# Input products of chunks 8 to 15 in two frames of 512 tokens, with the state inputs rotated in place

## The chip, the cores and the metric

The kernel runs on one core of one Trainium2 chip. The metric is device time in microseconds (us) of one execution; lower is better. The engines are PE (TensorE, matmuls), PEld (its weight loads), DVE (VectorE), ACT (ScalarE), POOL (GpSimd) and SP (SyncE, which starts transfers). Each works through its own queue in order. "L697" is line 697 of the kernel in question, so the same operation has different line numbers in different kernels. The granted clock is the share of TensorE's full clock that the chip allowed, as the profile records it. The record classes a run as slow when it is over 1.5% above the fastest of the same kernel.

## The reference, cut to what matters

```python
Bu = einsum("bld,pd->blp", layernorm(x), B_bar)     # L = 2048 tokens, D = P = 1024
for t in range(L):
    h = Lam_bar * h + Bu[:, t]                      # complex diagonal recurrence
y = 2 * einsum("blp,dp->bld", hs, C).real + layernorm(x) * Dskip
# ... plus: the two tokens with the highest x @ w_r go through a gated expert,
# y[those tokens] += sigmoid(r) * ((silu(xs @ w_gate) * (xs @ w_up)) @ w_down)
```

(Shortened: each branch is one line, the residual x + layernorm(x) is left out, and in the expert's line x is the normalised x, on which the kernel works.)

## The kernel before

The tokens are cut into 16 chunks of 128. For each chunk:

1. ScalarE normalises x (sum, sum of squares, rstd, apply). A transfer transposes it.
2. TensorE forms the input products u of a *frame* of two chunks: 8 groups, each of 16 matmuls of 256 columns. ScalarE moves each group from PSUM, where TensorE's results are written, into u: its *evacuation*.
3. VectorE rotates u into v, so that the complex recurrence becomes two real scans; scans v into gf (two buffers); ScalarE casts gf into gb, which frees gf; VectorE turns gb back into hT (the *turn back*).
4. TensorE forms the output products of hT; VectorE adds the residual (L863) and the chunk is stored.

In between, the router (r_bf and what follows it on VectorE) selects the two tokens, and TensorE runs the expert in 21 small steps, each with its own weights from HBM.

```python
def evac_u(f, j):                                    # ScalarE, one group of a frame of 2 chunks
    if j == 0:
        u_tiles[f] = work.tile([128, 2, PT, TF], BF16, name="u", bufs=2)
    nc.scalar.copy(out=u_tiles[f][:, :, j, :], in_=pB_tiles.pop((f, j))[:])

def turn_in(c, js=ALLJ):                             # VectorE, L697 to L699
    ...
    rot = v[:, :, js, 2:]
    nc.vector.tensor_tensor(out=rot, in0=u, in1=both(E1c, js), op=ALU.mult)
    nc.vector.tensor_tensor(out=m[:, :, js, :], in0=u[:, ::-1], in1=E1s[:, :, js, :], op=ALU.mult)
    nc.vector.tensor_add(out=rot, in0=rot, in1=m[:, :, js, :])

# scan, L718: v -> gf (two buffers); scan_out, L724, ScalarE: gf -> gb
```

The order of every queue is fixed when the program is built. A list scheduler in the kernel picks among the tasks that are ready by a priority key, and a long table `ADJUST` of hand-tuned shifts of these keys follows the kernel from version to version. So this change is also a change of the order on every engine.

## Time and profile before

| | before |
|---|---|
| time | 266.6 us (266.29 to 266.65) |
| profiled span | 264.4 us |
| busy: PE, DVE, ACT | 256.5, 251.5, 158.9 us |
| VectorE's waits of 0.3 us and more | 6.0 us, of which 2.3 at the start and 1.8 at the very end |
| granted TensorE clock | 1.0 |

How to read it: two engines have almost no free time, so neither can take up a delay of the other for long. From 20 to 258 us VectorE has no wait over 0.7 us. The prediction below shows the lines.

### The profile page before, as it was taken

To read this page: it belongs to the slowest core of one execution; us is meant where nothing else is said; L and a number is where in the kernel's file an instruction comes from. 1 tells how busy PE (TensorE), PEld (TensorE's weight loads), DVE (VectorE), ACT (ScalarE), POOL (GpSimd) and SP (SyncE) were. 2 spreads that over 40 slices of the span, in tenths; PEclk is the share of its full clock that TensorE was granted. 3 is DMA by queue.
4 is the path that set the end of the run, shared out by engine and by line. 5 is a ranking of instruction groups with operands and counts; after the bars stand their busy time and mean duration, and the time that the engine had idled before them with its cause. 6 is when DMAs were issued, how large, how long until landed. Compare 5 with 4: busy or idle time off the path is not lost.

```text
span 264.4 us, 5522 instructions
## 1 busy us (share of the span) xinstructions
PE 256.5 (97%) x2207; PEld 173.2 (66%) x2227; DVE 251.5 (95%) x334; ACT 158.9 (60%) x281; POOL 83.6 (32%) x126
## 2 busy tenths in 40 slices
PE   7799999999999999999999999999999999999994
PEld 7799988774688457456756586455864776644461
DVE  6999999999999999999999999999998999999992
ACT  3799999959699999996524447034551533145110
POOL 4221303563545440731040217115260409011100
PEclk9999999999999999999999999999999999999999
DMA  8999999998541125416111197588967884770411
GB/s 180 188 175 218 171 235 229 248 271 293 153 137 57 47 60 165 138 40 183 58 62 60 35 360 237 187 266 287 296 235 253 289 272 175 269 288 20 117 46 40
DMA packets 66165, 46.51 MB, mean 176 GB/s; under 512 B 45844, under 2 KB 52122, under 8 KB 66140
## 3 DMA queue, kind: packets, MB, share of 16 engines
q1 hardware_dynamic: 65788, 45.82, 63.4%
q8 instruction: 17, 0.28, 0.5%
q0 software_dynamic: 144, 0.27, 0.3%
q10 hardware_dynamic: 208, 0.07, 0.1%
q14 instruction: 8, 0.07, 0.1%
HBM read 30.94 MB, written 4.20 MB: 133 GB/s over the span
## 4 chain that ended last, share of the span: by engine, by line
PE 61%; DVE 28%; issue 3%; SPq 2%; ACT 2%; DMA 2%; DVEq 0%
PE pB L646 34%; PE pY L849 20%; DVE gf L718 9%; DVE ot L863 3%; PE pG L1048 3%; DVE hT L759 3%; DVE m L760 3%; DVE v L699 2%; DVE v L697 2%; DVE m L698 2%; DMA BT<-in_A_B_im_dram 2%; DVE gb L711 2%; SPq L286 2%; PE pD L1088 1%; PE pY L842 1%
## 5 line engine op out<-in xcount | busy, mean ns | idle before, releaser
L646 PE MATMUL pB<-xnT,BT 128*128 128x256 bf16 (+1 forms) x1104 | 117.5, 265 | 1.1 <-DMA BT<-in_A_B_im_dram 1.1
L849 PE MATMUL pY<-CT,hT 128*128 128x512 bf16 (+1 forms) x508 | 114.8, 372 | 1.7 <-issue 0.5
L646 PEld LDWEIGHTS <-BT 128*128 128x128 bf16 x1104 | 99.7, 98 | 16.2 <-issue 3.2
L849 PEld LDWEIGHTS <-hT 128*128 128x128 bf16 x528 | 49.1, 98 | 52.6 <-issue 3.2
L734 POOL TENSOR_TENSOR cw<-gf,tL 128x16 f32<-128x16 f32 (+1 forms) x38 | 35.0, 924 | 136.1 <-DVE gf L718 135.2
L718 DVE TENSOR_TENSOR_SCAN gf<-R,v 128x1040 f32<-128x1040 f32 (+1 forms) x38 | 69.0, 1851 | 0.2
L652 ACT CAST u<-pB 128x512 bf16<-128x512 f32 x64 | 36.5, 580 | 34.8 <-PE pB L646 34.7
L724 ACT CAST gb<-gf 128x1024 bf16<-128x1024 f32 (+1 forms) x38 | 32.4, 862 | 24.6 <-DVE gf L718 24.5
L810 ACT ACTIVATE xa<-xr,nmr_all,rstd_all 128x1024 f32<-128x1024 bf16 x12 | 14.9, 1239 | 21.9 <-DMA xr<-in_A_x_dram 8.1
L699 DVE TENSOR_TENSOR v<-v,m 128x2048 bf16<-128x2048 bf16 (+2 forms) x22 | 20.6, 938 | 0.8
L761 DVE TENSOR_TENSOR hT<-hT,m 128x2048 bf16<-128x2048 bf16 (+2 forms) x22 | 20.5, 934 | 0.8
L759 DVE TENSOR_TENSOR hT<-gb,E2c 128x2048 bf16<-128x2048 bf16 (+2 forms) x22 | 20.5, 930 | 0.2
L697 DVE TENSOR_TENSOR v<-u,E1c 128x2048 bf16<-128x2048 bf16 (+2 forms) x22 | 20.4, 928 | 0.2
L760 DVE TENSOR_TENSOR m<-gb,E2s 128x2048 bf16<-128x2048 bf16 (+2 forms) x22 | 20.5, 930 | 0.0
L698 DVE TENSOR_TENSOR m<-u,E1s 128x2048 bf16<-128x2048 bf16 (+2 forms) x22 | 20.4, 930 | 0.0
L863 DVE TENSOR_TENSOR ot<-pY,xa 128x512 bf16<-128x512 f32 (+1 forms) x25 | 16.0, 656 | 2.4 <-PE pY L852 1.8
L749 POOL CAST v<-cy 128x16 bf16<-128x16 f32 (+1 forms) x19 | 14.1, 744 | 1.4
L349 ACT ACTIVATE xn<-xt,nmean_all 128x1024 bf16<-128x1024 bf16 x12 | 13.8, 1149 | 0.3
L742 POOL TENSOR_TENSOR cy<-cw 128x16 f32<-128x16 f32 (+1 forms) x19 | 12.8, 674 | 1.5
L343 ACT ACTIVATE xn<-xt 128x1024 bf16<-128x1024 bf16 x12 | 12.6, 1054 | 0.0
L374 ACT ACTIVATE xn<-xt,nmr_all,rstd_all 128x1024 bf16<-128x1024 bf16 x10 | 12.4, 1241 | 0.3
L750 POOL TENSOR_TENSOR v<-cy,v 128x16 bf16<-128x16 f32 (+1 forms) x19 | 11.1, 586 | 1.5
(153 smaller groups left out, 186.6 us busy)
## 6 DMA issues: line engine op xcount, KB each, us to landing
wt<-in_B_w_up_dram SPq DMA_DIRECT2D x14, 512.0 KB, 5.1
wt<-in_B_w_gate_dram SPq DMA_DIRECT2D x14, 512.0 KB, 3.8
wt<-in_B_w_down_dram SPq DMA_DIRECT2D x14, 512.0 KB, 3.9
xt<-in_A_x_dram SPq DMA_DIRECT2D x16, 256.0 KB, 3.1
xr<-in_A_x_dram SPq DMA_DIRECT2D x16, 256.0 KB, 2.5
out_dram<-ot SPq DMA_DIRECT2D x31, 128.0 KB, 2.6
Drow<-in_A_Dskip_dram SPq DMA_DIRECT2D x1, 256.0 KB
xnT<-xn SPq DMA_TRANSPOSE x10, 2.8
```

The source lines that it names most:

```text
L646: nc.tensor.matmul(out=pB[:, ri, ts_], lhsT=BT[ri][j][:, k, :], rhs=xnT_tiles[f][:, k, ts_], start=(k == 0), stop=(k == DT - 1))
L652: nc.scalar.copy(out=u_tiles[f][:, :, j, :], in_=pB_tiles.pop((f, j))[:])
L697: nc.vector.tensor_tensor(out=rot, in0=u, in1=both(E1c, js), op=ALU.mult)
L698: nc.vector.tensor_tensor(out=m[:, :, js, :], in0=u[:, ::-1], in1=E1s[:, :, js, :], op=ALU.mult)
L699: nc.vector.tensor_add(out=rot, in0=rot, in1=m[:, :, js, :])
L718: nc.vector.tensor_tensor_scan(out=flat(gf), data0=flat(R[:, js, :]), data1=flat(v[:, ri, js, :]), initial=0.0, op0=ALU.mult, op1=ALU.add)
L724: nc.scalar.copy(out=gb_tiles[c][:, ri, js, :], in_=gf_tiles[c, js.start, ri][:, :, 2:])
L734: nc.gpsimd.tensor_tensor(out=cw_tiles[c, js.start][:, ri, :, 0:n], in0=g.unsqueeze(1).to_broadcast([128, 2, n]), in1=tL[:, ri, :, js], op ...
L759: nc.vector.tensor_tensor(out=rot, in0=g, in1=E2c[:, :, js, :], op=ALU.mult)
L760: nc.vector.tensor_tensor(out=m[:, :, js, :], in0=g[:, ::-1], in1=both(E2s, js), op=ALU.mult)
L849: nc.tensor.matmul(out=pY[:], lhsT=h_tiles[c][:, ri, j, :], rhs=CT[ri][h][:, j, d0:d0 + w], start=first and c in SKIP_DVE and ri == rs[0] ...
L863: nc.vector.tensor_add(out=y_tiles["ot", c][:, d_], in0=y_tiles.pop(("pY", c, dh))[:], in1=y_tiles["xa", c][:, d_])
```

## The change

The intent is to give TensorE longer matmuls (512 columns in place of 256, with half the weight loads) for the second half of the sequence. A frame of four chunks needs more of u at once. To make room, u and v are merged: six chunk slots, each written by ScalarE and rotated in place by VectorE; normalised x gets twelve chunk slots. Cut to its core:

```diff
-    CPF = TF // 128
+    CPF = 2
+    FRAMES = [(0, 1), (2, 3), (4, 5), (6, 7), (8, 9, 10, 11), (12, 13, 14, 15)]
+    NSLOT, NXS = 6, 12
...
+    u_all = work.tile([128, NSLOT, 2, PT, T + 2], BF16, name="u_all")
+    def stage_Bu1(f, j, ri):                         # 512 columns
+        for k in range(DT):
+            nc.tensor.matmul(out=pB[:], lhsT=BT[ri][j][:, k, :], rhs=xnT_all[:, k, x0:x0 + n], ...)
...
-        nc.vector.tensor_tensor(out=rot, in0=u, in1=both(E1c, js), op=ALU.mult)
         nc.vector.tensor_tensor(out=m[:, :, js, :], in0=u[:, ::-1], in1=E1s[:, :, js, :], op=ALU.mult)
-        nc.vector.tensor_add(out=rot, in0=rot, in1=m[:, :, js, :])
+        nc.vector.tensor_tensor(out=u, in0=u, in1=both(E1c, js), op=ALU.mult)
+        nc.vector.tensor_add(out=u, in0=u, in1=m[:, :, js, :])
...
-            cw_tiles[c, js.start] = small.tile([128, 2, 2, PT], F32, name="cw", bufs=3)
+            cw_tiles[c, js.start] = small.tile([128, 2, 2, PT], F32, name="cw", bufs=2)
...
 ADJUST = {                                           # every shift is new, among them:
+    ('gb', 5, 0, 0): 50.3, ('gb', 5, 0, 1): 150.6,
```

(Comments and "..." are mine; some 60 lines of shifts are left out.)

## The prediction

> **What bounds the kernel now.** I read the page first, then the chain that ended last in order of time, then the waits of VectorE, then VectorE's timeline. From the page, the busy times and the chain's shares:
>
> ```profile
> span 264.4 us, 5522 instructions
> PE 256.5 (97%) x2207; PEld 173.2 (66%) x2227; DVE 251.5 (95%) x334; ACT 158.9 (60%) x281; POOL 83.6 (32%) x126
> ...
> PE 61%; DVE 28%; issue 3%; SPq 2%; ACT 2%; DMA 2%; DVEq 0%
> ```
>
> TensorE and VectorE are both nearly full, and the chain changes between them: TensorE to about 59 us, VectorE from 66 to 118, TensorE to 232, VectorE to 258. So it is a balance of two full engines, and a saving on one alone is worth at most what the other has spare. What VectorE has spare is read from its waits:
>
> ```profile
> DVE ot L863 <- PE pY L852: 1.8, 2, 1.5
> DVE halfpi L237 <- PEq L1150: 0.8, 1, 0.8
> DVE st L334 <- DMA xt<-in_A_x_dram: 0.8, 1, 0.8
> DVE first_tok L243 <- POOL par_i L234: 0.7, 1, 0.7
> DVE guT L1077 <- PE pU L1068: 0.7, 1, 0.7
> DVE ot L863 <- PE pY L849: 0.5, 1, 0.5
> DVE row L918 <- PE pR L914: 0.4, 1, 0.4
> DVE E1s L615 <- ACT sf L545: 0.3, 1, 0.3
> ```
>
> Of these 6.0 us, 2.3 are the start, and 1.8 the last products at the end, which any order has. The rest, 0.7 + 0.5 + 0.4 + 0.3 = 1.9 us, is all that VectorE could give up. Its other 7 us of not-busy time (264.4 - 251.5 - 6.0) are the store after its last instruction (2.8 us) and small gaps between dependent instructions. Those gaps decide this case, and the timeline shows them:
>
> ```profile
> 101.09 2.31 DVE L718 TENSOR_TENSOR_SCAN gf<-R,v 128x1040 f32<-128x1040 f32 x1
> 103.32 1.26 DVE L863 TENSOR_TENSOR ot<-pY,xa 128x512 bf16<-128x512 f32 x2
> 104.50 2.31 DVE L718 TENSOR_TENSOR_SCAN gf<-R,v 128x1040 f32<-128x1040 f32 x1
> 106.85 1.23 DVE L697 TENSOR_TENSOR v<-u,E1c 128x2048 bf16<-128x2048 bf16 x1
> 107.99 1.25 DVE L698 TENSOR_TENSOR m<-u,E1s 128x2048 bf16<-128x2048 bf16 x1
> 109.27 1.23 DVE L699 TENSOR_TENSOR v<-v,m 128x2048 bf16<-128x2048 bf16 x1
> 110.41 1.22 DVE L759 TENSOR_TENSOR hT<-gb,E2c 128x2048 bf16<-128x2048 bf16 x1
> ```
>
> Columns: start, duration, engine, line, operation. An instruction that needs nothing of the one before starts before that one has ended: L698 comes 1.14 us after L697, although L697 lasts 1.23. One that needs it starts after its end: L699 comes 1.28 after L698 (1.25 to 1.26 in other chunks). A scan with an unrelated add behind it takes 2.23 us (101.09 to 103.32); a scan with a rotation behind it that overwrites the very v buffer just scanned takes 2.35 (104.50 to 106.85). The second pair carries no data from one to the other, only a buffer to be reused. So a wait on the instruction directly before costs about 0.12 us, whether for data or for a buffer.
>
> **What the Trainium skill says.** "TensorE: Matmul & The Clock Gate", section "Wait — 56ns, not 53.3ns?", gives a warm matmul of N columns a start-to-start time of N / 2.4 GHz plus about 2.5 ns. The trace agrees: in the chain 80 input products of 256 columns take 8.76 us, 109.5 ns each (formula 109.2), and 16 output products of 512 columns take 3.45 us, 215.6 ns each (formula 215.8). "VectorE: DVE Perf Modes", section "The DRAIN you can't avoid", says that a semaphore between two VectorE instructions costs nothing extra. This trace disagrees, by the 0.12 us above; I go by the trace. The section "Two Vector instructions with no wait between them" does say that unheld instructions may overlap. "Mode 2×_1P — pack two bf16 into one 32-bit read" asks for 4-byte alignment and step ±1; the new u slots begin at element 2 of rows of 130 bf16, so at 4 bytes, as v does already. L699, which reads and writes v in that layout, takes 1.22 us like the others, so I expect the in-place instructions to keep their durations.
>
> **The change, part by part.**
>
> TensorE. For chunks 8 to 15, 512 matmuls of 256 columns become 256 of 512. One pair saves 2 x 109.5 - 215.6 = 3.4 ns by the trace (2.5 by the formula): 256 pairs give 0.6 to 0.9 us. The 256 weight loads that vanish (98 ns each, 25 us of PEld) lay under matmuls of 109 ns and save nothing. Streamed columns are unchanged. Sum: -0.7 us.
>
> ScalarE. Still 64 evacuations of 512 elements (580 ns each). The normalisation of chunks up to 11 is now needed when frame 8 to 11 starts. In the kernel before, ScalarE wrote normalised chunk 11 at 91 us and chunk 15 at 117 us; the new order of ScalarE's queue puts chunk 11 behind nearly the same work, and I count frame 8 to 11 to start near 107 us on TensorE. So no wait there.
>
> VectorE. The number of instructions is the same (290 listed rows in both). What changes is who stands behind whom:
> - In the old rotation L697 wrote v and L698 read u: independent. In the new one the first instruction reads u into m, and the second overwrites u, so it must wait for the first. The built program has a wait on VectorE itself on this second instruction in all 22 rotations; it is always the direct neighbour. +22 waits.
> - m is now written by the first instruction, so it stands directly behind the last reader of m wherever a rotation follows another rotation or a turn back: 4 + 2 places. Before, an instruction lay between. +6.
> - A scan directly behind its own rotation: 4 places before, 6 now. +2.
> - The old rotation that waits for the scan just before it to free v: 6 places with such a wait. With six slots gone. -6.
> Sum: 24 waits of 0.12 us = 2.9 us more on VectorE.
>
> Buffers. Six slots instead of two u frames and two v buffers remove waits which the trace does not show anyway. The coarse frame asks for something instead: the first rotation of chunks 12 to 14 must follow all 16 groups of their frame. I summed both queues in their new order with the durations of this trace. From the first group of that frame, TensorE has 16 x 8 x 0.2156 = 27.6 us of it, with eight expert products between (8 x 0.55 = 4.4) and one small transpose pair: 32 us, from about 161 to 193.6. VectorE comes to chunk 12 at about the same time, 193.6. With 0.7 us for the evacuation it waits up to about 0.8 us there, where before it had a like wait of 0.7 for guT. Frame 8 to 11 ends about 137 us, a microsecond ahead of VectorE. After chunk 12 is ready, VectorE has 67 us of work and TensorE 64, so VectorE is the later one. These times are estimates, good to a microsecond or two.
>
> Sum on the path: VectorE +2.9, less what of its 1.9 us of waits the new order may avoid (I take 0.5); TensorE's 0.7 us falls on the engine that finishes earlier and is lost. 264.4 + 2.4 = 266.8 us of span, plus the 2.2 us between span and time (266.6 - 264.4): 269.0 us.
>
> **Rivals.**
> 1. TensorE is the bound and only its saving counts: 266.6 - 0.7 = 265.9, and with the waits of VectorE smoothed out by the new order perhaps 264.5. For it: 97% busy against 95%, and 61% of the chain. Against: the chain's last 26 us before the final products are VectorE's, and the trace shows less than 2 us that it could give up, so it cannot take up 2.9 us unseen.
> 2. The coarse frames open a new hole: VectorE waits for frame 12 to 15, or TensorE waits for evacuations that wait for the scan of chunk 9. If TensorE is late by 3 us at chunk 12, VectorE's remaining work ends 3 us later: 272. For it: my two sums meet within a microsecond. Against: the new order starts chunk 15's first parts before chunk 12, which need only 8 and 12 of the 16 groups, so whoever ordered it had seen this place.
> 3. The in-place waits cost only when VectorE is on the path. If half of them fall where TensorE is late, +1.4 and about 267.5. Against: VectorE has no gap over 0.7 us between 20 and 258 us, so a delay anywhere is carried to the end.
>
> **Range and chances.** Rival 1 gives the low side, rival 2 the high one. An order that was evidently searched anew for this kernel leans to the low side of my sum: I take 266.0 to 271.8. Faster by over 2% would be under 261.3; VectorE's own 251.5 busy, 2.3 start and 4.6 end leave a span of 258.4, a time of 260.6, as a floor with no gap at all: 2%. Slower by over 2% is over 271.9, needs rival 2: 9%. The rest, 89%.
>
> **What would show it.** Right: in the changed kernel's timeline the second instruction of every rotation starts 1.25 us or more after the first (before: 1.14), durations unchanged near 1.22; 512-column products 215 to 217 ns apart; VectorE in the chain for most of the last 70 us; TensorE with new idle time in the tail. Wrong: if the second instruction still starts at 1.14, my main cost is none; if VectorE's durations rise, the slots' layout costs; if VectorE waits over 2 us for input products, rival 2; if the span falls below 264, TensorE was the bound.

## The result, and the profile after

The time rose to 276.2 us (275.30 to 277.14, four runs), against 266.6. The ratio is 1.0367 (95%: 1.0332 to 1.0402). A ratio here is the mean time of one kernel's fast runs over that of the other's of the same rounds, so not quite the ratio of the medians quoted. The prediction said 269.0, at most 271.8.

The page of the kernel after, first lines and the chain's shares:

```profile
span 273.7 us, 5046 instructions
...
PE 257.5 (94%) x1971; PEld 147.9 (54%) x1971; DVE 253.5 (93%) x334; ACT 159.2 (58%) x281; POOL 80.9 (30%) x126
...
PE 51%; DVE 32%; ACT 5%; issue 5%; DMA 3%; SPq 2%; DVEq 0%
```

The span grew by 9.3 us, but TensorE's busy time by 1.0 and VectorE's by 2.0. The rest is waiting. VectorE's waits in the kernel after (waiter, line, what it waited for: us in total, times, longest):

```profile
DVE gf L753 <- ACT gb L759: 3.8, 2, 2.6
DVE ot L895 <- PE pY L884: 2.7, 2, 2.3
DVE hT L794 <- ACT gb L759: 1.6, 2, 1.1
DVE guT L1109 <- PE pU L1100: 1.1, 1, 1.1
...
DVE m L732 <- ACT u_all L680: 0.6, 2, 0.3
```

Two rows are new in kind: 3.8 + 1.6 = 5.4 us of waits for ScalarE's casts gf to gb, which the kernel before does not have. VectorE's timeline shows where (start, duration, engine, line, operation; in brackets the wait before it):

```profile
104.11 1.20 DVE L732 TENSOR_TENSOR m<-u_all,E1s 128x2048 bf16<-128x2048 bf16 x1
105.35 1.22 DVE L733 TENSOR_TENSOR u_all<-u_all,E1c 128x2048 bf16<-128x2048 bf16 x1
106.61 1.22 DVE L734 TENSOR_TENSOR u_all<-u_all,m 128x2048 bf16<-128x2048 bf16 x1
...
111.53 2.31 DVE L753 TENSOR_TENSOR_SCAN gf<-R,u_all 128x1040 f32<-128x1040 f32 x1
115.02 2.33 DVE L753 TENSOR_TENSOR_SCAN gf<-R,u_all 128x1040 f32<-128x1040 f32 x1 [1.18 <-ACT gb L759]
118.46 1.23 DVE L794 TENSOR_TENSOR hT<-gb,E2c 128x2048 bf16<-128x2048 bf16 x1 [1.11 <-ACT gb L759]
...
122.00 2.32 DVE L753 TENSOR_TENSOR_SCAN gf<-R,u_all 128x1040 f32<-128x1040 f32 x1
126.91 2.33 DVE L753 TENSOR_TENSOR_SCAN gf<-R,u_all 128x1040 f32<-128x1040 f32 x1 [2.60 <-ACT gb L759]
```

The first three lines are the in-place rotation: its second instruction starts 1.24 us after the first (104.11 to 105.35); before, it was 1.14. Over the 11 rotations of this size the medians are 1.25 and 1.13 us, and over all 22 rotations the difference sums to 2.5 us. Three of the last five lines carry new waits; a fourth, of 0.53 us, is at 96.13. ScalarE's timeline says why the cast for the last one was late:

```profile
118.33 1.55 ACT L680 CAST u_all<-pB 128x512 bf16<-128x512 f32 x3
119.76 1.08 ACT L356 ACTIVATE xn<-xt 128x1024 bf16<-128x1024 bf16 x1
...
123.55 1.24 ACT L387 ACTIVATE xn<-xt,nmr_all,rstd_all 128x1024 bf16<-128x1024 bf16 x1
...
124.88 1.05 ACT L680 CAST u_all<-pB 128x512 bf16<-128x512 f32 x2
125.82 1.05 ACT L759 CAST gb<-gf 128x1024 bf16<-128x1024 f32 x1
```

The cast at 125.82 is that of chunk 5's second scan, which had ended 21.6 us earlier, at 104.2 (101.90 + 2.30). It stands in ScalarE's queue behind the evacuations of frame 8 to 11 and the normalisation of chunk 15. The Trainium skill's page "TensorE: Matmul & The Clock Gate", section "Architectural detail: the array is 16× 32×32, not 1× 128×128", says that the queues of ScalarE and VectorE are strict FIFO. The trace agrees: the cast's input had been ready for 21.6 us, and it did not overtake. Until it came, one of the two gf buffers was held, and both scans of chunk 6 and the first of chunk 7 shared the other; the built program shows the same address for these three. The late place is no accident of the run. It is the shift 150.6 in the diff above: built with 50.3 in its place (not run), the scheduler puts this cast directly behind that of the first half.

The last view is the end of the two kernels, in windows. The columns are the window, its length, then busy us and instructions of PE, PEld, DVE, ACT and POOL, the granted clock, the DMA share and GB/s. Before:

```profile
220.00:240.00 20.00, 19.79 (x179) 10.38 (x179) 19.83 (x21) 6.92 (x10) 6.13 (x9) 1.00 0.64 227
240.00:258.00 18.00, 17.80 (x103) 9.20 (x103) 17.60 (x27) 4.45 (x5) 1.59 (x1) 1.00 0.20 60
```

After:

```profile
220.00:240.00 20.00, 17.66 (x125) 7.50 (x127) 19.67 (x17) 6.61 (x7) 9.16 (x10) 1.00 0.82 274
240.00:258.00 18.00, 15.39 (x122) 7.10 (x122) 17.77 (x17) 6.30 (x9) 4.50 (x5) 1.00 0.38 123
```

Before, both engines are full up to the end, because the input products of chunks 14 and 15 run as late as 207 to 227 us, between output products and expert steps. After, all input products are done at 198.7, and TensorE has only work that waits for VectorE: it is idle for 2.3 + 2.6 us here.

As sums on VectorE the 9.3 us come out like this. Lost overlap takes 2.9 (2.0 of busy time that used to overlap, and 0.9 of gaps under 0.2 us); 2.5 of it are the in-place waits. The waits for casts take 5.4, chunk 12 takes 0.8 (1.14 + 0.34 in place of 0.67 before), the end 0.9 (2.7 for 1.8), and the other waits, some new and some gone, -0.6. That makes 9.4, within rounding. The experiments show that such a sum is not yet an explanation.

### The profile page after: what moved, and what is told of

It reads as the page before. It is cut to its first block, busy times and chain, and to the rows that moved or that the text cites. A ratio compares the mean times of both kernels' runs of the same rounds, so it can differ in the third digit from the quotient of the medians.

```text
span 273.7 us, 5046 instructions
## 1 busy us (share of the span) xinstructions
PE 257.5 (94%) x1971; PEld 147.9 (54%) x1971; DVE 253.5 (93%) x334; ACT 159.2 (58%) x281; POOL 80.9 (30%) x126
## 4 chain that ended last, share of the span: by engine, by line
PE 51%; DVE 32%; ACT 5%; issue 5%; DMA 3%; SPq 2%; DVEq 0%
PE pY L881 22%; PE pB L677 14%; DVE gf L753 12%; PE pB L661 10%; DVE m L795 3%; DVE hT L794 3%; PE pG L1080 3%; DVE u_all L733 3%; DVE m L732 2%; DVE u_all L734 2%; DMA BT<-in_A_B_im_dram 2%; SPq L300 2%; DVE hT L796 2%; DVE ot L892 2%; ACT gb L759 2%
## 5 line engine op out<-in xcount | busy, mean ns | idle before, releaser
L881 PE MATMUL pY<-CT,hT 128*128 128x512 bf16 (+1 forms) x528 | 117.4, 373 | 2.3 <-DVE ot L892 2.3
L753 DVE TENSOR_TENSOR_SCAN gf<-R,u_all 128x1040 f32<-128x1040 f32 (+1 forms) x38 | 69.4, 1854 | 3.9 <-ACT gb L759 3.8
L661 PE MATMUL pB<-xnT_all,BT 128*128 128x256 bf16 (+1 forms) x592 | 58.9, 258 | 2.0 <-ACT u_all L669 1.2
L677 PE MATMUL pB<-xnT_all,BT 128*128 128x512 bf16 x256 | 58.2, 379 | 0.0
L661 PEld LDWEIGHTS <-BT 128*128 128x128 bf16 x592 | 50.7, 98 | 7.9 <-issue 1.3
L677 PEld LDWEIGHTS <-BT 128*128 128x128 bf16 x256 | 23.9, 98 | 30.3 <-issue 3.6
L680 ACT CAST u_all<-pB 128x512 bf16<-128x512 f32 x32 | 18.2, 584 | 16.3 <-PE pB L677 16.3
L733 DVE TENSOR_TENSOR u_all<-u_all,E1c 128x2048 bf16<-128x2048 bf16 (+2 forms) x22 | 20.6, 936 | 0.8
L734 DVE TENSOR_TENSOR u_all<-u_all,m 128x2048 bf16<-128x2048 bf16 (+2 forms) x22 | 20.5, 934 | 0.8
L732 DVE TENSOR_TENSOR m<-u_all,E1s 128x2048 bf16<-128x2048 bf16 (+2 forms) x22 | 20.3, 924 | 1.0 <-ACT u_all L680 0.6
L669 ACT CAST u_all<-pB 128x512 bf16<-128x512 f32 x32 | 18.0, 578 | 2.4 <-PE pB L661 2.3
L874 PE MATMUL pY<-dgD,xnT_all 128*128 128x128 bf16 x96 | 9.5, 219 | 4.6 <-DVE ot L892 2.6
```

Source lines behind the costliest of these rows:

```text
L661: nc.tensor.matmul(out=pB[:, ri, ts_], lhsT=BT[ri][j][:, k, :], rhs=xnT_all[:, k, x0 + ts_.start:x0 + ts_.stop], start=(k == 0), stop=(k = ...
L677: nc.tensor.matmul(out=pB[:], lhsT=BT[ri][j][:, k, :], rhs=xnT_all[:, k, x0:x0 + n], start=(k == 0), stop=(k == DT - 1))
L733: nc.vector.tensor_tensor(out=u, in0=u, in1=both(E1c, js), op=ALU.mult)
L734: nc.vector.tensor_add(out=u, in0=u, in1=m[:, :, js, :])
L753: nc.vector.tensor_tensor_scan(out=flat(gf), data0=flat(R[:, js, :]), data1=flat(v[:, ri, js, :]), initial=0.0, op0=ALU.mult, op1=ALU.add)
L881: nc.tensor.matmul(out=pY[:], lhsT=h_tiles[c][:, ri, j, :], rhs=CT[ri][h][:, j, d0:d0 + w], start=first and c in SKIP_DVE and ri == rs[0] ...
```

## The experiments

Each edit is to the kernel after unless said otherwise. "Over before" is (ratio - 1) x 266.5 us, so kernels of different sessions can be compared; that of the kernel after is 9.8 us.

| run | edit | median us | ratio to before (95%) | over before |
|---|---|---|---|---|
| after | | 276.23 | 1.0367 (1.0332 to 1.0402) | 9.8 |
| e1 | cast of chunk 5 early | 274.69 | 1.0294 (1.0273 to 1.0314) | 7.8 |
| e2 | no in-place waits | 274.19 | 1.0302 (1.0283 to 1.0320) | 8.0 |
| e3 | both | 271.95 | 1.0215 (1.0194 to 1.0236) | 5.7 |
| e4 | kernel before, with in-place waits | 269.05 | 1.0091 (1.0073 to 1.0110) | 2.4 |
| e5 | last frame in two | 276.34 | 1.0370 (1.0336 to 1.0404) | 9.9 |
| e6 | e5, chunk 5's cast and turn back early | 274.00 | 1.0287 (1.0262 to 1.0311) | 7.6 |
| e7 | e6, no in-place waits | 272.69 | 1.0244 (1.0218 to 1.0270) | 6.5 |
| e8 | 512-column matmuls split | 276.93 | 1.0377 (1.0350 to 1.0404) | 10.0 |
| e9 | storage alone | 268.59 | 1.0088 (1.0073 to 1.0103) | 2.3 |
| e10 | storage alone, no in-place waits | 266.35 | 1.0005 (0.9991 to 1.0019) | 0.1 |
| e11 | e7, expert steps later | 272.82 | 1.0253 (1.0231 to 1.0275) | 6.7 |
| e12 | e11 with the last frame of four | 275.78 | 1.0361 (1.0333 to 1.0390) | 9.6 |
| e13 | plain order, frames 4+4 | 293.90 | 1.1033 (1.0981 to 1.1086) | 27.5 |
| e14 | plain order, frames 2+2+2+2 | 273.25 | 1.0271 (1.0249 to 1.0292) | 7.2 |
| e15 | plain order, frames 4+2+2 | 288.88 | 1.0866 (1.0826 to 1.0906) | 23.1 |
| e16 | plain order, frames 2+2+4 | 293.52 | 1.1026 (1.0990 to 1.1062) | 27.3 |

All outputs were correct.

One caution. The times of the kernel after fall into two groups, 275.3 to 275.5 and 276.9 to 277.1, and so do those of e1 (273.8, and 274.7 to 274.8), e5 and e8. The profiles of e1 and e8 are of the longer group. In them the granted clock falls for some us near 250 (in e1 to 0.85 and 0.80 in the windows 245 to 250 and 250 to 255; that of e8 is shown at the end), and VectorE then has one more wait for output products (0.94 us each, at 261.1 and 263.6). The profile of the kernel after, of the shorter group, shows neither. So tables of waits from profiles of different groups can differ by about 1 us in this row. Over whole runs the mean clock of the kernel after is 0.990 to 0.996, that of the kernel before 0.996 to 1.0. What this costs was not measured apart.

### e1 to e4: casts, in-place waits, and whether waits add up

Two theories were set against each other: SUM (every wait of VectorE counts in full) and RELAY (different engines set the pace in different stages, so a wait counts only where its engine does).

e1 moves one task in the built order; nothing else changes its place on its engine:

```diff
+    o.remove(('gb', 5, 0, 1))
+    o.insert(o.index(('gb', 5, 0, 0)) + 1, ('gb', 5, 0, 1))
```

> The kernel after, every engine's order kept, but ScalarE casts the second half of chunk 5's scan directly behind the first half, 20 us earlier. In the profile after, that cast came at 125.82, and until it came one of the two gf buffers was held: both scans of chunk 6 and the first of chunk 7 had to share the other. Expected in the trace under every theory: the waits of VectorE at 115.02 (1.18 us) and 126.91 (2.60 us) gone, 3.8 us together. For the time: theory SUM (VectorE is the bound all along, each of its waits counts in full) says 3.8 us less than after's 276.2, about 272.4. Theory RELAY (TensorE runs without a pause from 132.9 to 199 and VectorE waits for it at chunk 12, so VectorE's gain before 127 reaches the end only as far as TensorE's pause of 1.9 us before 132.9 goes) says 274.3, with VectorE's wait at chunk 12 grown from 1.5 to about 3 us. Rival FRAMES (the loss is the coarse frames and the casts are only where it shows) says no change, 276.

e2 gives the first product a place of its own, in slots that are dead at that time:

```diff
+        m2 = <two dead slots of xnT_all, or slot 0 of u_all for chunks 8 and 10>
+        nc.vector.tensor_tensor(out=m2, in0=u, in1=both(E1c, js), op=ALU.mult)
         nc.vector.tensor_tensor(out=m[:, :, js, :], in0=u[:, ::-1], in1=E1s[:, :, js, :], op=ALU.mult)
-        nc.vector.tensor_tensor(out=u, in0=u, in1=both(E1c, js), op=ALU.mult)
-        nc.vector.tensor_add(out=u, in0=u, in1=m[:, :, js, :])
+        nc.vector.tensor_add(out=u, in0=m2, in1=m[:, :, js, :])
```

> The kernel after, order kept, but the rotation writes u*E1c into a scratch (slots of xnT and u that are dead at the time) instead of over u, with the instruction order of the kernel before; the 22 waits of the second instruction on the first go. Expected in the trace: start to start 1.14 instead of 1.25 us. For the time: SUM says 22 x 0.12 = 2.6 us less, 273.6. RELAY says only the rotations after chunk 12's wait count (12, 13, 14 and the last part of 15: 4 x 0.12 = 0.5 us), as up to 127 us ScalarE's queue and from 133 to 199 TensorE set the pace: about 275.6.

e3 is both edits.

> Both edits. SUM: 3.8 + 2.6 = 6.4 us less, 269.8. RELAY: 1.9 + 0.5 = 2.4 us less, 273.8, and VectorE's wait at chunk 12 grows to 4 us or more.

e4 is an edit of the kernel *before*:

```diff
-        nc.vector.tensor_tensor(out=rot, in0=u, in1=both(E1c, js), op=ALU.mult)
         nc.vector.tensor_tensor(out=m[:, :, js, :], in0=u[:, ::-1], in1=E1s[:, :, js, :], op=ALU.mult)
-        nc.vector.tensor_add(out=rot, in0=rot, in1=m[:, :, js, :])
+        nc.vector.tensor_tensor(out=u, in0=u, in1=both(E1c, js), op=ALU.mult)
+        nc.vector.tensor_add(out=rot, in0=u, in1=m[:, :, js, :])
```

> The kernel before, with one thing of the change: the rotation reads u into m first, then multiplies u by E1c in place, then writes v = u + m, so the second instruction waits for the first in all 22 rotations; v is written one instruction later, which relaxes 6 waits on the scan before. The prediction's own main term, alone. SUM: 22 x 0.12 - 6 x 0.12 = 1.9 to 2.6 us more than 266.6, so 268.5 to 269.2. RELAY: in the chain of the kernel before VectorE sets the pace only from 66 to 118 us and after 232, in which lie the rotations 5 to 7 and the last part of 15: 0.4 to 0.6 us more, about 267.1.

The in-place waits behaved as SUM says. e4 adds them to the kernel before (and relaxes 6 waits of v on the scan before) and costs 2.4 us. Its timeline (the rotation of chunk 7):

```profile
107.68 1.20 DVE L697 TENSOR_TENSOR m<-u,E1s 128x2048 bf16<-128x2048 bf16 x1
108.91 1.22 DVE L698 TENSOR_TENSOR u<-u,E1c 128x2048 bf16<-128x2048 bf16 x1
```

The second instruction starts 1.23 us after the first, where the kernel before has 1.14. By the medians (1.25 and 1.13) it is 0.12 us; over all 22 rotations the difference is again 2.5 us. Taking them away in the kernel after (e2) gains 1.8 us, nearer to SUM's 2.6 than to RELAY's 0.5. So RELAY was wrong about them: VectorE sets the pace in more places than I had thought, above all before 95 us. The waits for casts are as long as in the kernel after, but come 2.0 us earlier (the turn back of chunk 4 at 94.11 in place of 96.13).

The cast did not behave as SUM says. e1 removes a wait of 1.18 and one of 2.60 us, and gains 2.0. VectorE's waits in e1 show where the rest went:

```profile
DVE ot L895 <- PE pY L884: 3.7, 3, 2.5
DVE hT L794 <- ACT gb L759: 3.1, 2, 2.6
DVE guT L1109 <- PE pU L1100: 1.1, 1, 1.1
...
DVE m L732 <- ACT u_all L680: 0.8, 2, 0.5
```

The row for gf is gone, as expected, but the row for hT has grown from 1.6 to 3.1. The turn back of chunk 6 now comes earlier and waits for its own cast, which stands behind the same normalisations. The row for ot has grown from 2.7 to 3.7; the new wait in it is the one of 0.94 us after the fall of the clock. At chunk 12 VectorE still waits 1.1 + 0.3 us for TensorE. So RELAY had the gain (1.9 expected) but not the mechanism: it expected about 3 us of waiting at chunk 12, and the wait there did not grow. (In e2 and e3 it grew to 1.9 + 0.3.) e3 gains 4.1 us, about the two gains together (2.0 + 1.8), and leaves 5.7 us over the kernel before.

### e5 to e8: the last coarse frame, and the gain of the long matmuls

e5 keeps the 16 places of the last frame's groups, but fills them with two frames of two, and moves two rotations:

```diff
     def stage_Bu1(f, j, ri):
+        if f in PAIRED:                              # PAIRED = (5,): chunks 12 to 15
+            return stage_pair(f, 2 * j + ri)         # groups 0 to 7: chunks 12, 13; 8 to 15: chunks 14, 15
...
+    for n in (('TI', 13, 0), ('TI', 12, 0)):         # rotations of 12 and 13
+        behind(n, ('SC', 11, 0, 1))                  # directly behind the last scan of chunk 11
```

> The kernel after with frame 12 to 15 alone undone: in the places of its 16 groups of 512 tokens TensorE first does the 8 groups of chunks 12 and 13 (two times 256 columns each), then the 8 of chunks 14 and 15, and VectorE takes the rotations of 12 and 13 directly behind the last scan of 11, before the two early parts of 15. Storage, casts and frame 8 to 11 stay. Expected in the trace: no wait of VectorE for guT and u_all near 199 (1.14 + 0.34 us in after). RELAY (VectorE waits for TensorE at chunk 12, and its work after that sets the end): 1.5 us less than after's 276.2, 274.7. SUM says the same 1.5. Rival CASTS ALONE (only the casts and the in-place waits matter, TensorE is never the later one): no change.

e6 adds e1's move and one more:

```diff
+    behind(('gb', 5, 0, 1), ('gb', 5, 0, 0))
+    behind(('TO', 5, 0), ('cw', 6, 0))               # turn back of chunk 5 behind the scans of chunk 6
```

> Run e1's earlier cast, with the turn back of chunk 5 moved on VectorE to between the second scan and the turn back of chunk 6 (its data are there, and the cast of chunk 6 gets 3.5 us), and with e5's frame of two. e1 by itself gave 1.5 to 2 us of the 3.8, as a wait of 2.6 for the cast of chunk 6 took the place of the others and VectorE then still waited 1.5 at chunk 12. RELAY: with the frame of two VectorE's gain is no longer lost there: 5.4 - 0.5 (the casts) + 1.5 (chunk 12) = 6.4 us less, 269.8. If the frame does not matter: e1 plus 1.5, about 273. If TensorE is at its own bound from 84 us on: about 272.

e7 adds e2's scratch.

> e6 with the scratch of e2 as well (no in-place waits). e2 and e3 showed the scratch to be worth 2.0 to 2.6 us, and adding the waits to the kernel before cost 2.4. Sum: 269.8 - 2.4 = 267.4, less than 1 us above the kernel before: then the three causes (casts 4.9, in-place waits 2.4, coarse last frame 1.5) account for the whole 9.7 us. If something else of the change costs, the rest stays over 269.

e8 splits each 512-column matmul in two of 256, with nothing else changed:

```diff
+        for h in (0, n // 2):
-        for k in range(DT):  matmul(out=pB[:], ..., rhs=xnT_all[:, k, x0:x0 + n])
+            for k in range(DT):  matmul(out=pB[:, h:h + n // 2], ..., rhs=xnT_all[:, k, x0 + h:x0 + h + n // 2])
```

> The kernel after with each 512-column input product split into two of 256 columns, frames and order kept: the one saving of the change, taken away. In the trace TensorE spends 256 x 3.4 ns = 0.9 us more in them. RELAY: 128 of them lie between 132.9 and 199, where TensorE sets the pace, 0.4 us more; those before lie in front of TensorE's pause of 1.9 us and cost nothing: 276.6. VectorE the bound throughout: no change, 276.2. TensorE the bound throughout: 277.1.

e5 gained nothing, and e6 and e7 stayed 4 and 5 us above the expectation. The waits for casts and the wait at chunk 12 did go, but others took their places. VectorE in e7:

```profile
127.58 0.17 DVE L966 CAST r_bf<-r_ps 128x16 bf16<-128x16 f32 x1 [2.06 <-PE r_ps L437]
...
129.48 0.21 DVE L974 COPY row<-pR 16x128 bf16<-16x128 bf16 x1 [1.13 <-PE pR L970]
...
203.84 0.42 DVE L1117 TENSOR_TENSOR mw<-mw,pG 128x256 f32<-128x256 f32 x1 [2.33 <-ACT mw L1112]
```

The router now waits for TensorE, which has the last of the router's products behind ten groups of frame 8 to 11. At 203.84 the expert's gate waits for ScalarE, which itself waits for an expert step that TensorE starts at 201.77. So VectorE's waits are moved along, not removed, wherever TensorE has the needed product behind a block of input products. My expectation for e5 to e7 had treated chunk 12 as the one place where VectorE meets TensorE. That was wrong.

e8 prices the intended gain. Its 512 matmuls of 256 columns take 58.7 us of TensorE, against 58.2 for the 256 of the kernel after. The time is 0.2 us longer, well inside the intervals: the saving is not to be seen in the time. From groups of instructions, e8 and then the kernel after (line, operation, tiles, count | busy us, mean ns | idle before):

```profile
L678 PE MATMUL pB<-xnT_all,BT 128*128 128x256 bf16 x512 | 58.7, 273 | 0.0
```

```profile
L677 PE MATMUL pB<-xnT_all,BT 128*128 128x512 bf16 x256 | 58.2, 379 | 0.0
```

### e9 and e10: the storage alone

e9 keeps the storage of the kernel after, but sets all frames to two chunks and takes every engine's order from the kernel before:

```diff
-    FRAMES = [(0, 1), (2, 3), (4, 5), (6, 7), (8, 9, 10, 11), (12, 13, 14, 15)]
+    FRAMES = [(c, c + 1) for c in range(0, 16, 2)]
...
-    pl.run().emit()
+    pl.order = <the order of the kernel before, task by task>
+    pl.emit()
```

The twelve slots of x are handed out so that this order's reuse holds: chunks 8 to 11 take those of 0 to 3, and 12 to 15 the last four.

> The other side of the change: the kernel after with its storage (six slots of u rotated in place, twelve of normalised x, two small carry buffers in place of three), but with all frames of two and with every engine's order of the kernel before. If the storage costs only its in-place waits (theory STORAGE IS CHEAP, ORDER COSTS THE REST): run e4 put these at 2.4 us, so 266.4 + 2.4 = 268.8, and no wait for casts near 115 to 127. If the storage itself brings the rest (its layout, waits of the evacuations for the scans of six chunks before, fewer carry buffers): 272 to 276.

e10 adds the scratch of e2, in slots that are dead in this order.

> e9 with the product u*E1c in dead slots of normalised x, in the instruction order of the kernel before: the storage without in-place waits. Expected 266.4 or a little less: the waits on the scan that freed v, 6 x 0.12 = 0.7 us, are gone as well, so 265.7 if all of them lay on the path. This is also the candidate to beat both kernels.

These two split the change. The storage costs 2.3 us (e9), as much as the in-place waits alone in e4, and without these waits it costs nothing (e10: 0.1 us, interval -0.2 to +0.5). The waits of evacuations for scans six chunks back, the new layout of u and the two carry buffers are together free in this order. Of the 0.7 us that the old waits on v might have given back, nothing is to be seen. The page of e10 suggests why VectorE's gains end here:

```profile
PE 256.5 (97%) x2207; PEld 173.3 (66%) x2227; DVE 251.2 (95%) x334; ACT 158.8 (60%) x281; POOL 83.7 (32%) x126
...
PE 82%; DVE 12%; DMA 4%; issue 1%; ACT 0%; SPq 0%
```

TensorE is 97% busy and carries 82% of the chain. It has no more to give in this order. So 9.8 - 2.3 = 7.5 us of the loss belong to the frames of four and the order made for them; e9 does not tell these two apart.

### e11 and e12: the expert steps

e11 moves the gate product and the copy behind it (gu and gT of blocks 2 and 3) some instructions later on VectorE; e12 is the same with the last frame of four, as in the change:

```diff
+    behind(('gu', 2), ('TI', 14, 0))
+    behind(('gT', 2), ('TO', 11, 0))
+    behind(('gu', 3), ('xa', 9))
+    behind(('gT', 3), ('ADD', 9, 0))
```

> e7 (casts, frame of two for 12 to 15, scratch) with the expert steps on VectorE (gu and guT of blocks 2 and 3) moved some instructions later. e5 to e7 did not gain from the frame of two: VectorE took chunk 12 without a wait, but then stood 1.4 to 2.3 us at the expert's gate product, because TensorE reaches the expert products late (the router's result comes 4 to 9 us later than in the kernel before). With that step later in VectorE's order its 2.3 + 0.5 us should go: 272.7 - 2.8 = 269.9. If TensorE sets the pace at this place whatever VectorE's order is, another wait takes its place: 272 or more.

> e11 with the frame of four for 12 to 15 left as the change has it. The difference of the two is what the coarse last frame costs once nothing else stands in its way. RELAY: VectorE waits for the 16th group at chunk 12, 2 to 3 us, so 272 to 273 against e11's 269.9. If the frame is innocent: the same time as e11.

e11 missed: 272.8 against an expected 269.9. The wait of 2.33 us went, but 0.7 and 1.0 us appeared at the next expert steps. e12 is 2.9 us slower than e11, but it is not the clean test of the frame that I had meant. In it TensorE waits 2.4 us for the very gate product that I had moved. The two together say only that single moves do not mend this order.

### e13 to e16: frames of two and four in the plain order

What was left open was whether frames of four cost in themselves, or only in this tuned order. So all the tuned shifts were taken out:

```diff
-ADJUST = { ... }                                     # some 60 lines
+ADJUST = {}
```

The list scheduler then orders the tasks by its plain keys, and only FRAMES differs between the four.

> The kernel after with every hand-tuned shift of keys removed: the list scheduler's plain order, frames of four for 8 to 11 and 12 to 15. FRAMES (a block of 27.6 us of input products costs in any order): at least 4 us longer than the same with frames of two. ORDER (the frames are innocent, the tuned order was a poor one): within 2 us of e14.

> The same plain order with frames of two throughout, storage of the kernel after. FRAMES: the fastest of the four. Without its shifts it should be slower than e9 (268.6, the same frames and storage in the tuned order of before).

> Frame of four for 8 to 11 only, frames of two for 12 to 15. FRAMES: between e13 and e14; if the first coarse frame is the costly one (it presses the normalisation of chunks 10 and 11 on ScalarE forward and pushes casts back, as in the kernel after at 95 to 127 us), near e13.

> Frames of two for 8 to 11, frame of four for 12 to 15. FRAMES: between e13 and e14; if the last coarse frame is the costly one (all products of 12 to 15 done before VectorE's chunk 12, TensorE idle in the tail), near e13. ORDER: all four within 2 us.

The frames of four cost 20 us in the plain order (27.5 against 7.2 over before). Either one alone costs nearly as much (16 and 20), so the two do not add up. And e14, with no tuning at all, is 3 us *faster* than the tuned kernel after. VectorE in e13, where e14 has no wait over 0.35 us from 132 to 195:

```profile
139.92 0.23 DVE L906 COPY sel_scr<-pI 128x64 f32<-128x64 f32 x1 [2.54 <-PE pI L902]
...
145.21 0.69 DVE L831 TENSOR_TENSOR ot<-pY,xa 128x512 bf16<-128x512 f32 x1 [2.19 <-PE pY L817]
...
153.38 0.54 DVE L959 TENSOR_SCALAR xnsel<-xsel,mv,rstd_s 2x1024 bf16<-2x1024 bf16 x1 [4.95 <-ACT rstd_s L264]
...
158.61 1.22 DVE L668 TENSOR_TENSOR m<-u_all,E1s 128x2048 bf16<-128x2048 bf16 x1 [1.78 <-ACT u_all L616]
```

While TensorE does the block of frame 8 to 11, VectorE has only the router and single adds, and each of the waits shown is for something that stands among the groups of that block on TensorE, or among their evacuations on ScalarE. The last line is the first rotation of the frame, at 158.6. Later TensorE waits: 12.4 us for turns back (0.4 in e14), and 6.4 us for transfers of expert weights, which e14 does not have. (e15 does not have them either and still loses 16 us, so they are not needed for the loss.) From TensorE's timeline in e13:

```profile
236.42 0.39 PE L1056 MATMUL pD<-wt,guT 128*2 128x256 bf16 x8 [0.93 <-DMA wt<-in_B_w_down_dram]
239.03 0.39 PE L1056 MATMUL pD<-wt,guT 128*2 128x256 bf16 x8 [2.22 <-DMA wt<-in_B_w_down_dram]
242.43 0.59 PE L1056 MATMUL pD<-wt,guT 128*2 128x256 bf16 x8 [3.02 <-DMA wt<-in_B_w_down_dram]
246.51 5.12 PE L817 MATMUL pY<-CT,hT 128*128 128x512 bf16 x15 [3.48 <-DVE hT L732]
```

Its clock falls too. The busy rows of TensorE and its granted clock in e13, in 40 slices of 7.3 us:

```profile
PE   6999999699999999999999988999999941939795
...
PEclk9999999899999999999999999999999995888999
```

After the slice with 40% busy comes one with 10%, and in it the clock falls to 0.5, with 0.8 in the three slices that follow. The Trainium skill's page "TensorE: Matmul & The Clock Gate", section "HAM oscillation — how this bites in real kernels", warns of idle gaps of more than about 3.4 us for this reason. The trace agrees that pauses go with a lower clock, but not on the length: the clock was down from 239.7 to 250.0 us (mean from 240 to 250: 0.50), so it fell after pauses of 0.9 and 2.2 us, 0.3 us into that of 3.0 and before that of 3.5. What the transfers and the clock add to the 20 us was not measured apart from the frames.

## Why the prediction was wrong, point by point

- *The in-place waits, +2.9 us.* Right. The 22 waits sum to 2.5 us in the trace; in the time they cost 2.4 (e4) or 2.3 (e9) by themselves, and 1.8 as a part of the whole (e2). The term was a little too large. The smaller counts in it (+6, +2, -6) were not tested one by one.
- *TensorE's saving, 0.7 us, lost.* Right in kind: 0.5 us less busy (e8), nothing in the time.
- *Durations of the slots' layout unchanged.* Right: 1.20 to 1.23 us.
- *"So no wait there"*, of ScalarE. **This step failed.** It asked only whether normalised chunk 11 is in time for TensorE. It did not ask what the same, earlier evacuations and normalisations push back in an in-order queue: the casts that free gf and feed the turns back. These cost 5.4 us in the trace. In the time, the late cast of chunk 5 alone cost about 2 (e1; 2.3 on top of e2), and with the turn back of chunk 5 moved too, again 2.3 (e6 against e5). The shift that puts one of them 21 us late was in the diff and I did not read it.
- *Rival 2, the coarse frames, given 9%, and the part "Buffers".* **This step failed too.** The frames, with the order made for them, were the larger half, and I looked for their cost in one place only, chunk 12. My estimate for the end of the last frame was 193.6 us; it was 198.7. At chunk 12 itself VectorE waited just 1.5 us, and removing that alone gained nothing (e5). In the traces the cost is spread: the frames move TensorE's input products in front of everything else that VectorE waits for (the router's product, expert steps) and leave TensorE idle at the end, where VectorE still has its turns back. After the in-place waits (2.3) and the late cast (about 2), some 5.5 us of the 9.8 are left for this. That coarse frames cost is shown for the plain order (e13 against e14). That the 5.5 us in the tuned order are of the same kind is argued from its trace (waits that come back one step later in e6, e7 and e11), not shown by a run that removes them.
- *"An order that was evidently searched anew for this kernel leans to the low side."* Wrong, as e14 shows. The tuned shifts improve frames of four from 293.9 to 276.2, but the plain order with frames of two takes 273.3.
- *Right/wrong signs.* The 1.25 us, the unchanged durations, the 216 ns of the 512-column products and the idle time of TensorE in the tail came as named. "VectorE in the chain for most of the last 70 us" did not: after 200 us the chain is mostly TensorE's to 222, VectorE's from 226 to 253.7, and TensorE's again to 270. TensorE had paused 2.34 and 2.26 us at 238 and 249 and then had 16 us of products left. I had named its idle time as a sign of being right; it was part of the loss. The prediction named "VectorE waits over 2 us for input products" as the sign of rival 2. The sign that came was VectorE waiting for other things that stand behind input products, which I had not listed.

What stays open: whether a better order for frames of four exists. No run shows one. The best found with them is e3, at 5.7 us over before. No version beat both kernels; e10 equals the kernel before within its interval.

## What to carry to other kernels

When a change makes the unit of work on one engine coarser, ask for every in-order queue what the earlier-needed work will stand in front of, and not only whether that work itself is in time. A sum of waits in one trace says where time went and not what comes back: 3.8 us of waits removed gave 2.0, and three further removals gave little, since another engine had the same thing behind the same block. Split a mixed change (storage, granularity, order) by giving the new storage the old order: two runs here settled what eight moves of single instructions had not.

## What the Trainium skill lacked or had wrong

- Page "VectorE: DVE Perf Modes", section "The DRAIN you can't avoid", says, of a series of eight copies, that the semaphore costs nothing extra. Here a wait on the instruction directly before, for a buffer and not for data, costs 0.12 us: 1.25 us from start to start against 1.13 (medians of the full rotations), and 22 such waits added to a kernel on VectorE's pace cost 2.4 us (e4).
- Page "TensorE: Matmul & The Clock Gate", section "HAM oscillation — how this bites in real kernels", speaks of idle gaps over about 3.4 us. In e8 the clock fell with shorter ones. After pauses of TensorE of 2.35 and 2.26 us, with 2.74 us of work in the five before, the next 5 us had a clock of 0.66. The kernel after has pauses of 2.34 and 2.26 us in the same places, and in its profile the clock stayed at 1.00 there; so the length of a pause alone does not decide it. The windows of e8, with the columns of those above:

```profile
245.00:250.00 5.00, 2.74 (x28) 1.26 (x27) 4.87 (x5) 3.81 (x6) 4.46 (x5) 1.00 0.02 9
250.00:255.00 5.00, 5.00 (x19) 2.01 (x18) 4.97 (x6) 0.95 (x2) 0.00 (x0) 0.66 0.24 84
```
